# Twelve float32 units for eighteen, eight weight blocks ahead for fourteen, and two small operations moved to other engines

## The chip, the cores and the metric

The kernel runs on one core of one Trainium2 chip. The metric is the device time in microseconds (us). Every number of the profile is of one profiled execution of the kernel before; engines are named TensorE (PE; its weight loads PEld), VectorE (DVE), ScalarE (ACT), GpSimd (POOL) and SyncE (SP), which issues most transfers.

## The reference

Attention with a sliding window and a few sinks, then a two-layer feed-forward over its output:

```python
def _attn_ref(q, k, v, n_sink, window):        # (4, 8, 768, 64); 4 sinks, window 128
    scores = scale * np.matmul(q, k.transpose(0, 1, 3, 2))
    keep = is_sink | in_window                  # pos_k < n_sink, or 0 <= pos_q - pos_k < window
    scores = np.where(keep, scores, -1000000000.0)
    a = np.exp(scores - np.max(scores, axis=-1, keepdims=True))
    a = a / (np.sum(a, axis=-1, keepdims=True) + 1e-09)
    return np.matmul(a, v)

def _moe_ref(x, w_in, w_out):                   # (3072, 512) @ (512, 2048), @ (2048, 512)
    h = x @ w_in
    g = np.where(h >= 1, h, np.where(h <= -1, 0.0, (h + 1) ** 2 / 4))
    return g @ w_out
```

All arrays are float32, except that the weights come as 64-bit floats, which the kernel decodes itself.

## The kernel before

**Units and chunks.** A unit is one batch, one head and three blocks of 128 queries: 64 units in all. Eight units (the heads of one batch and one half of the sequence) make a chunk, whose 384 rows of attention output, `xn`, are the input of one feed-forward. There are eight chunks. While the feed-forward of one chunk runs, the units of the next go through attention. The first stage therefore has attention alone, the last feed-forward alone.

**A unit's four steps** follow each other in the list that `attn_steps` makes, one unit behind the next. `load` fetches q and k. `scores` makes three score blocks of 128 x 260 (two neighbouring key blocks and four sinks), takes their row maxima on VectorE (L236, the custom operation, with the mask) and the exponential with the sums on ScalarE (L239); then it adds 1e-9 to the three sums (L244), takes the reciprocal (L245) and scales the rows (L257 on ScalarE, L259 on VectorE). `transp` transposes the probabilities on TensorE (L312, L314; L324, L325) and copies them back. `av` multiplies them by v (L378). `values` fetches v.

**Two kinds of units.** The first `NATIVE` = 18 units are "native": q, k, probabilities and v are plain float32, which TensorE takes in two rows per matmul. The others are split for float32r: each number is written as a rounded high part (ScalarE: L214, L217, L283, L288) and a remainder (a subtraction: L216, L218, L284, L289), and the matmul is done with both. L218, L284 and L289 are on GpSimd; the remainder of k, L216, is on VectorE, but on GpSimd for the units in `KL_POOL`. Split units add the previous block's probabilities (L251), form the remainder of the transposed probabilities (L329, L331), mask it into two triangles on GpSimd (L334, L336: the affine selections), spread the sinks (L338), and add two halves of the output (L383, L384). Native units need none of this; instead they have a second group of transposes, more rows in `av`, and a copy of the transposed sinks (L320).

**Weights.** 32 blocks (w_in and w_out in turn, 128 x 512 each) are fetched as 64-bit words and decoded by four rows on VectorE (L147, L148, L149, L151) and one on ScalarE (L150). The first `WFIRST` = 14 blocks are interleaved with the first stage, in the list that the program is written from; the other 18 with the first feed-forward.

**The feed-forward** goes through 16 blocks of 128 hidden columns: `stage1` (L416, 12 matmuls), the activation (L423, L424 on ScalarE, L425 on VectorE, L426 on ScalarE, then the remainder `gl`, L427: on GpSimd in the first feed-forward, on VectorE in the others), and `stage2` (L435, 9 matmuls), which runs `LAG` = 2 blocks behind. Its input is split by L446 (ScalarE) and L447 (VectorE), four quarters each.

**What sets the order.** TensorE's rows stand in the order written by `spread`, which interleaves attention and feed-forward by estimated weights. On VectorE, ScalarE, GpSimd and SP a scheduler sets the order; each engine then works through its queue strictly in that order, so a row that waits holds up all behind it.

Of the kernel before, what the change touches and what calls it, by code (L numbers as in the profile page):

```python
# [13 lines left out]
ALU = mybir.AluOpType  # L14
# [3 lines left out]
P = 128  # L18
NT = S // P
CT = 3  # L20
NSINK = 4
# [2 lines left out]
QK = CT * P + P + CT * KB  # L24
NJ = DFF // P

NATIVE = 18


KL_POOL = range(18, 20)  # L30
GL_POOL = 0
NORM = "vaa"


CHECK = range(24, 24 + 2 * NJ)
WFIRST = 14
AHEAD = 3
SYNC = 8

# [10 lines left out]
def attn_ffn(ctx, tc, qk, vx, vs, par, w_in, w_out, out):  # L50
    nc = tc.nc
# [64 lines left out]
    for r0 in (0, 32):  # L116
        r = r0 + CT * NSINK
# [77 lines left out]
    def load(u):  # L195
        b, h, t0 = u
        T = CT * P
        W = (P if t0 else -NSINK) + CT * KB
        if units.index(u) < NATIVE:

# [13 lines left out]
        nc.scalar.copy(k_s, k_r)  # L214
        eng = nc.gpsimd if units.index(u) in KL_POOL else nc.vector
        eng.tensor_tensor(k_s[D:P], k_r[D:P], k_s[D:P].bitcast(F32), op=ALU.subtract)  # L216
# [4 lines left out]
    def scores(u, i):  # L221
        b, h, t0 = u
        qs, k_s = st["qk", u]
        if i == 0:
            st["p", u] = [att.tile([P, CT, 260], F32, name="p"), att.tile([P, 2 * CT], F32, name="stat")]
        p, stat = st["p", u]
        t = t0 + i
        lo = KB if t == 0 else 0
        c0 = i * KB if t0 else max(0, (i - 1) * KB)
        ps = ps_a.tile([P, 512], F32, name="ps_a")  # L230
        for j, q in enumerate(qs):
            nc.tensor.matmul(ps[:, lo:260], lhsT=q[:, i * P:(i + 1) * P], rhs=k_s[:, c0:c0 + 260 - lo],  # L232
                             start=(j == 0), stop=(j == len(qs) - 1))
        peak_i = peak[:, units.index(u), i:i + 1]
        m = m0 if t == 0 else (m1 if t == 1 else m2)
        nc.vector.tensor_tensor_reduce(  # L236
            out=p[:, i, lo:260], in0=ps[:, lo:260], in1=m, scale=-0.0625 if units.index(u) < NATIVE else -0.125, scalar=3.0e38,
            op0=ALU.add, op1=ALU.min, accum_out=peak_i)
        nc.scalar.activation(p[:, i, lo:260], p[:, i, lo:260], AF.Exp, bias=peak_i, scale=-1.0,  # L239
                             accum_out=stat[:, i:i + 1])  # L240
        if i < CT - 1:
            return
        st.pop(("qk", u))
        nc.vector.tensor_scalar(stat[:, CT:2 * CT], stat[:, 0:CT], 1.0e-9, None, op0=ALU.add)  # L244
        nc.vector.reciprocal(stat[:, CT:2 * CT], stat[:, CT:2 * CT])  # L245
        i0 = int(t0 == 0)
        c0 = 0
        if units.index(u) >= NATIVE:

            c0 = P  # L250
            nc.vector.tensor_tensor(p[:, i0:, KB:260], p[:, i0:, KB:260], p[:, i0:, 0:P], op=ALU.add)  # L251
        for i in range(CT):
            lo = KB if t0 + i == 0 else c0
            r = stat[:, CT + i:CT + i + 1]
            eng = NORM[i] if units.index(u) < NATIVE else "v"
            if eng == "a":
                nc.scalar.activation(p[:, i, lo:260], p[:, i, lo:260], AF.Copy, scale=r)  # L257
            else:
                (nc.gpsimd if eng == "p" else nc.vector).tensor_scalar(p[:, i, lo:260], p[:, i, lo:260], r, None,  # L259
                                                                       op0=ALU.mult)  # L260
        if units.index(u) < NATIVE:
            sk = None
        else:
            sk = att.tile([P, CT * NSINK], F32, name="sk")[:, :(CT - i0) * NSINK]
            nc.vector.tensor_copy(sk.rearrange("p (i s) -> p i s", s=NSINK), p[:, i0:, P:KB])
        st["p", u] = (p, sk)

    def values(u):
        b, h, t0 = u
        kb0 = max(t0 - 1, 0)  # L270
        nb = t0 + CT - kb0
        if units.index(u) < NATIVE:
            v_s = att.tile([P, 4, 2, D], F32R, name="v_s").bitcast(F32).rearrange("p n a d -> p (n a) d")[:, :nb]
# [19 lines left out]
    def transp(u, part):  # L293
# [4 lines left out]
        ns = CT - i0  # L298
        r = ns * NSINK
        spt = sp[units.index(u) % 2]  # L300
        ps = ps_a.tile([P, 512], F32, name="ps_a")
# [6 lines left out]
        if units.index(u) < NATIVE:  # L308
            c, blk = ((0, 0), (1, KB))[part]
            i0 = i0 * (1 - part)  # L310
            for i in range(i0, CT):
                nc.tensor.transpose(ps[:, i * P:(i + 1) * P], p[:, i, blk:blk + P], ident)  # L312
                if not part:
                    nc.tensor.transpose(ps[:NSINK, (i - 1) * CT * P:((i - 1) * CT + 1) * P], p[:, i, P:KB], ident)  # L314
            nc.scalar.copy(pth.bitcast(F32)[:, i0:, c], ps[:, i0 * P:T].rearrange("p (i q) -> p i q", q=P))  # L315
            if part:
                st.pop(("p", u))
            else:
                spt = st["sp", u] = spn[units.index(u) % 2]
                nc.vector.tensor_copy(spt[:NSINK].rearrange("r (t q) -> r t q", q=P)[:, :ns],  # L320
                                      ps[:NSINK].rearrange("r (t q) -> r t q", q=P)[:, ::CT])
            return
        for i in range(CT):
            nc.tensor.transpose(ps[:, i * P:(i + 1) * P], p[:, i, KB:260], ident)  # L324
# [181 lines left out]
    ps = ps_a.tile([P, 512], F32, name="ps_a")  # L506
# [56 lines left out]
    with tc.If(other_v > 0):  # L563
        with tc.tile_pool(name="gen", bufs=1) as gen:
# [9 lines left out]
            for t0 in (0, CT):  # L574
                keep = gen.tile([P, CT, S], F32, name="keep")
                kidx = gen.tile([P, S], I32, name="kidx")
                r = gen.tile([P, S], F32, name="r")
# [53 lines left out]
```

## Time and profile before

| | us |
|---|---|
| median of 3 runs (742.02 to 743.75) | 743.18 |
| the profiled execution | 744.81 |
| its span, first to last instruction | 743.0 |
| TensorE matmuls busy (3867 rows) | 709.9 |
| VectorE busy (1456 rows) | 535.2 |
| ScalarE busy (1301 rows) | 505.0 |
| GpSimd busy (446 rows) | 267.9 |

The page's chain of waits (the work that ended last, followed back) gives TensorE 61% of the span, VectorE 20%, ScalarE 8%. The busy time of matmuls is modelled at its end, so a TensorE at 100% can still hide short waits. In the 40 slices of the span (18.6 us each) the busy tenths are

```profile
PE   5889999999999999999989999999999999999996
DVE  7998994346877787878877888878888677842221
ACT  4887776566767877777767876778676675544342
POOL 2101312313544454535445454645545444410000
```

A digit is the busy share of a slice in tenths. The first feed-forward matmul starts at 61.4 us, the second feed-forward's at 157.4.

### The profile page before, as it was taken

What the parts mean: (1) busy time and instruction counts of PE and PEld (TensorE: products, weight loads), DVE (VectorE), ACT (ScalarE), POOL (GpSimd) and SP (SyncE); (2) the same over time, 40 slices, a digit from 0 to 9 for tenths busy, and PEclk for the clock granted to TensorE, in tenths of its full rate; (3) what the DMA queues carried; (4) which work ended last, traced back from release to release, by engine and by line L of the source; (5) the groups of instructions that cost most, each with busy time, mean ns of one, the idle gap of its engine ahead of it and who ended that gap; (6) DMA issues with size and microseconds to landing.
All of it is one profiled execution on the core that took longest, in us unless ns stands there. A gap on an engine that the chain in (4) does not pass through costs nothing.

```text
span 743.0 us, 12353 instructions
## 1 busy us (share of the span) xinstructions
PE 709.9 (96%) x3867; PEld 622.9 (84%) x3867; DVE 535.2 (72%) x1456; ACT 505.0 (68%) x1301; POOL 267.9 (36%) x446
## 2 busy tenths in 40 slices
PE   5889999999999999999989999999999999999996
PEld 3446888888998998999879998899888999989995
DVE  7998994346877787878877888878888677842221
ACT  4887776566767877777767876778676675544342
POOL 2101312313544454535445454645545444410000
PEclk9999999999999999999999999999999999999999
DMA  8876541221232443434424433415322120001001
GB/s 271 279 242 222 199 132 59 55 70 41 58 104 77 145 123 112 122 100 128 123 73 123 149 105 95 121 64 166 123 84 67 61 81 26 9 1 44 1 0 48
DMA packets 43211, 76.20 MB, mean 103 GB/s; under 512 B 7298, under 2 KB 27778, under 8 KB 43138
## 3 DMA queue, kind: packets, MB, share of 16 engines
q1 hardware_dynamic: 39682, 62.75, 27.4%
q10 hardware_dynamic: 3456, 12.58, 4.9%
q8 instruction: 33, 0.54, 0.3%
q14 instruction: 40, 0.33, 0.2%
HBM read 69.02 MB, written 6.29 MB: 101 GB/s over the span
## 4 chain that ended last, share of the span: by engine, by line
PE 61%; DVE 20%; ACT 8%; DMA 4%; issue 3%; POOL 2%; SPq 0%; ACTq 0%; POOLq 0%
PE o_ps L435 24%; PE h_ps L416 24%; PE ps_a L378 6%; PE ps_a L232 3%; DVE k_s L216 3%; DVE p L259 3%; ACT p L239 2%; DVE gl L427 2%; ACT k_s L214 2%; DVE pt L329 1%; DMA r<-qk 1%; DVE p L251 1%; DVE g L425 1%; DVE p L236 1%; PE ps_a L324 1%
## 5 line engine op out<-in xcount | busy, mean ns | idle before, releaser
L416 PE MATMUL h_ps<-x,wi 128*128 128x384 f32 x1536 | 311.1, 341 | 0.6 <-DVE x L447 0.6
L416 PEld LDWEIGHTS h_ps<-x,wi 128*128 128x128 f32 x1536 | 263.1, 188 | 10.5 <-issue 1.9
L435 PE MATMUL o_ps<-w,gh 128*128 128x512 f32 x768 | 244.5, 399 | 0.0
L435 PE MATMUL o_ps<-w,gl 128*128 128x512 f32 x384 | 151.2, 394 | 0.0
L435 PEld LDWEIGHTS o_ps<-w,gh 128*128 128x128 f32 x768 | 134.5, 188 | 16.6 <-issue 1.9
L425 DVE SCALAR_TENSOR_TENSOR g<-g,h_ps 128x384 f32<-128x384 f32 x128 | 70.2, 548 | 70.4 <-ACT g L424 69.8
L239 ACT ACTIVATE p<-p,peak 128x260 f32<-128x260 f32 (+1 forms) x192 | 94.0, 490 | 35.5 <-DVE peak L236 34.4
L423 ACT ACTIVATE g<-h_ps,half 128x384 f32<-128x384 f32 x128 | 73.7, 576 | 57.7 <-PE h_ps L416 56.4
L426 ACT CAST gh<-g 128x384 fp32r<-128x384 f32 x128 | 65.5, 511 | 60.7 <-DVE g L425 59.8
L218 POOL TENSOR_TENSOR q_l<-r,q_h 128x384 fp32r<-128x384 f32 x46 | 46.8, 1018 | 129.8 <-ACT q_h L217 123.0
L236 DVE CUSTOM_DVE_ANT_0 p<-ps_a,m 128x260 f32<-128x260 f32 (+1 forms) x192 | 74.2, 398 | 20.9 <-PE ps_a L232 19.9
L435 PEld LDWEIGHTS o_ps<-w,gl 128*128 128x128 f32 x384 | 72.0, 188 | 17.6 <-POOL gl L427 0.2
L427 DVE TENSOR_TENSOR gl<-g,gh 128x384 fp32r<-128x384 f32 x112 | 67.9, 606 | 26.1 <-ACT gh L426 25.2
L232 PE MATMUL ps_a<-k_s,q_h 128*128 128x260 f32 (+1 forms) x246 | 70.2, 335 | 15.7 <-DVE sk L331 7.6
L216 DVE TENSOR_TENSOR k_s<-k_r,k_s 64x524 fp32r<-64x524 f32 (+1 forms) x44 | 47.5, 1079 | 44.2 <-ACT k_s L214 44.2
L378 PE MATMUL ps_a<-pt,v_s 128*128 128x256 f32 (+2 forms) x402 | 69.9, 298 | 1.8 <-ACT pt L315 1.2
L232 PEld LDWEIGHTS ps_a<-k_s,q_h 128*128 128x128 f32 x246 | 45.5, 198 | 30.5 <-issue 11.4
L424 ACT ACTIVATE g<-g 128x384 f32<-128x384 f32 x128 | 67.1, 524 | 2.8
L336 POOL TENSOR_SCALAR_AFFINE_SELECT pt<-pt 128x384 fp32r<-128x384 f32 (+1 forms) x92 | 51.5, 560 | 45.0 <-DVE pt L329 36.4
L378 PEld LDWEIGHTS ps_a<-pt,v_s 128*128 128x128 f32 (+1 forms) x402 | 57.8, 176 | 11.7 <-issue 1.6
L259 DVE TENSOR_SCALAR p<-p,stat 128x132 f32<-128x132 f32 (+1 forms) x156 | 60.4, 433 | 0.3
L334 POOL TENSOR_SCALAR_AFFINE_SELECT pt<-pt 128x384 fp32r<-128x384 f32 (+1 forms) x92 | 49.1, 534 | 30.2 <-ACT pt L328 30.2
(108 smaller groups left out, 899.4 us busy)
## 6 DMA issues: line engine op xcount, KB each, us to landing
r<-qk SPq DMA_DIRECT2D x46, 192.0 KB
k_r<-qk SPq DMA_DIRECT2D x32, 262.0 KB
again<-w_in SPq DMA_DIRECT2D x16, 512.0 KB
again<-w_out SPq DMA_DIRECT2D x16, 512.0 KB
w<-w_in ACTq DMA_DIRECT2D x12, 512.0 KB
w<-w_out ACTq DMA_DIRECT2D x12, 512.0 KB
out<-o SPq DMA_DIRECT2D x23, 256.0 KB
r<-vx SPq DMA_DIRECT2D x32, 128.0 KB
```

The lines of the kernel that those rows point to most:

```text
L216: eng.tensor_tensor(k_s[D:P], k_r[D:P], k_s[D:P].bitcast(F32), op=ALU.subtract)
L232: nc.tensor.matmul(ps[:, lo:260], lhsT=q[:, i * P:(i + 1) * P], rhs=k_s[:, c0:c0 + 260 - lo], start=(j == 0), stop=(j == len(qs) - 1))
L236: nc.vector.tensor_tensor_reduce(out=p[:, i, lo:260], in0=ps[:, lo:260], in1=m, scale=-0.0625 if units.index(u) < NATIVE else -0.125, scal ...
L239: nc.scalar.activation(p[:, i, lo:260], p[:, i, lo:260], AF.Exp, bias=peak_i, scale=-1.0, accum_out=stat[:, i:i + 1])
L259: (nc.gpsimd if eng == "p" else nc.vector).tensor_scalar(p[:, i, lo:260], p[:, i, lo:260], r, None, op0=ALU.mult)
L378: nc.tensor.matmul(z, lhsT=w, rhs=y, start=(n == 0), stop=(n == len(mms) - 1))
L416: nc.tensor.matmul(h_ps[:, :T], lhsT=w_i[j][:, w, ct * P:(ct + 1) * P], rhs=x[:, y, ct], start=(ct == 0 and n == 0), stop=(ct == NCT - 1 a ...
L423: nc.scalar.activation(g, h_ps[:, :T], AF.Relu, bias=half, scale=0.5)
L424: nc.scalar.activation(g, g, AF.Square)
L425: nc.vector.scalar_tensor_tensor(g, g, 1.0, h_ps[:, :T], op0=ALU.min, op1=ALU.max)
L427: (nc.gpsimd if row0 == GL_POOL else nc.vector).tensor_tensor(gl, g, gh.bitcast(F32), op=ALU.subtract)
L435: nc.tensor.matmul(o_ps[tt], lhsT=gg[:, tt * P:(tt + 1) * P], rhs=w_o[j][:, w], start=(j == 0 and n == 0), stop=(j == NJ - 1 and n == 2))
```

## The change

Four edits. `NATIVE` falls from 18 to 12, so units 12 to 17 are split for float32r. `KL_POOL` becomes the range 12 to 18, so the remainder of k of those six units is on GpSimd, and that of units 18 and 19 moves to VectorE. `WFIRST` falls from 14 to 8, so in the written list six more blocks are decoded during the first feed-forward. The copy of the transposed sinks, L320, goes from VectorE to ScalarE, and the addition of 1e-9, L244, from VectorE to GpSimd, for all 64 units.

```diff
--- before.py
+++ after.py
@@ -24,16 +24,16 @@
 QK = CT * P + P + CT * KB
 NJ = DFF // P
 
-NATIVE = 18
-
-
-KL_POOL = range(18, 20)
+NATIVE = 12
+
+
+KL_POOL = range(12, 18)
 GL_POOL = 0
 NORM = "vaa"
 
 
 CHECK = range(24, 24 + 2 * NJ)
-WFIRST = 14
+WFIRST = 8
 AHEAD = 3
 SYNC = 8
 
@@ -241,7 +241,7 @@
         if i < CT - 1:
             return
         st.pop(("qk", u))
-        nc.vector.tensor_scalar(stat[:, CT:2 * CT], stat[:, 0:CT], 1.0e-9, None, op0=ALU.add)
+        nc.gpsimd.tensor_scalar(stat[:, CT:2 * CT], stat[:, 0:CT], 1.0e-9, None, op0=ALU.add)
         nc.vector.reciprocal(stat[:, CT:2 * CT], stat[:, CT:2 * CT])
         i0 = int(t0 == 0)
         c0 = 0
@@ -317,8 +317,8 @@
                 st.pop(("p", u))
             else:
                 spt = st["sp", u] = spn[units.index(u) % 2]
-                nc.vector.tensor_copy(spt[:NSINK].rearrange("r (t q) -> r t q", q=P)[:, :ns],
-                                      ps[:NSINK].rearrange("r (t q) -> r t q", q=P)[:, ::CT])
+                nc.scalar.copy(spt[:NSINK].rearrange("r (t q) -> r t q", q=P)[:, :ns],
+                               ps[:NSINK].rearrange("r (t q) -> r t q", q=P)[:, ::CT])
             return
         for i in range(CT):
             nc.tensor.transpose(ps[:, i * P:(i + 1) * P], p[:, i, KB:260], ident)
```

**VectorE, end of the first stage**, up to the last of the four quarters of the feed-forward's input (L447). `stat` are the sums, `spn` the sinks, `p` the probabilities, `peak` the maxima, `o` and `wi`/`w` the decode's words and results. Before:

```order
L245 RECIPROCAL stat_681<-stat_681 128x3
L320 COPY spn0_141<-ps_a_708 4x256
L147 TENSOR_SCALAR o_863<-w_699 128x512
L236 ISA p_735,peak_100<-ps_a_737,m0_111 128x128
L236 ISA peak_100 128x1
L259 TENSOR_SCALAR p_680<-p_680,stat_681 128x128
L151 TENSOR_TENSOR w_808<-o_809,w_808 128x512
L148 SCALAR_TENSOR_TENSOR o_863<-w_699,o_863 128x512
L236 ISA p_735,peak_100<-ps_a_761,m1_110 128x260
L236 ISA peak_100 128x1
L147 TENSOR_SCALAR o_925<-w_741 128x512
L447 TENSOR_TENSOR x_727<-xn_167,x_727 128x384
```

and now:

```order
L148 SCALAR_TENSOR_TENSOR o_944<-w_826,o_944 128x512
L245 RECIPROCAL stat_639<-stat_639 128x3
L151 TENSOR_TENSOR w_909<-o_910,w_909 128x512
L149 SCALAR_TENSOR_TENSOR o_944<-w_826,o_944 128x512
L259 TENSOR_SCALAR p_638<-p_638,stat_639 128x128
L236 ISA p_684,peak_100<-ps_a_686,m0_111 128x128
L236 ISA peak_100 128x1
L147 TENSOR_SCALAR o_979<-w_866 128x512
L236 ISA p_684,peak_100<-ps_a_713,m1_110 128x260
L236 ISA peak_100 128x1
L447 TENSOR_TENSOR x_676<-xn_167,x_676 128x384
```

The rows L244 and L320 are gone from the queue; the block decoded last in front of L447 is `w_808`, the sixteenth, before, and `w_909`, the fourteenth, now. The reciprocal L245 now follows a row of GpSimd.

**GpSimd, start of the first feed-forward.** `gl` are the remainders of the activation, one for each of the 16 blocks; `k_s`, `q_l` are the remainders of a unit's k and q. Before, the queue is:

```order
L427 TENSOR_TENSOR gl_785<-g_783,gh_784 128x384
L427 TENSOR_TENSOR gl_834<-g_832,gh_833 128x384
L427 TENSOR_TENSOR gl_855<-g_853,gh_854 128x384
L427 TENSOR_TENSOR gl_944<-g_942,gh_943 128x384
L427 TENSOR_TENSOR gl_1001<-g_999,gh_1000 128x384
L427 TENSOR_TENSOR gl_1072<-g_1070,gh_1071 128x384
```

and now:

```order
L244 TENSOR_SCALAR stat_639<-stat_639 128x3
L216 TENSOR_TENSOR k_s_849<-k_r_848,k_s_849 64x392
L218 TENSOR_TENSOR q_l_846<-r_851,q_h_847 128x384
L244 TENSOR_SCALAR stat_685<-stat_685 128x3
L427 TENSOR_TENSOR gl_725<-g_723,gh_724 128x384
L427 TENSOR_TENSOR gl_772<-g_770,gh_771 128x384
L427 TENSOR_TENSOR gl_812<-g_810,gh_811 128x384
L216 TENSOR_TENSOR k_s_1009<-k_r_1008,k_s_1009 64x392
L218 TENSOR_TENSOR q_l_1006<-r_1011,q_h_1007 128x384
L244 TENSOR_SCALAR stat_861<-stat_861 128x3
L427 TENSOR_TENSOR gl_886<-g_884,gh_885 128x384
L427 TENSOR_TENSOR gl_955<-g_953,gh_954 128x384
```

The subtractions of the first split units and the additions to their sums stand among the gl rows; the first gl comes behind the q and k of unit 12 and the sums of unit 10.

**GpSimd, a unit of a later stage** (L176 is a one-element copy that holds back a fetch of the weights for a later check; `pt` are transposed probabilities). Before:

```order
L218 TENSOR_TENSOR q_l_5135<-r_5140,q_h_5136 128x384
L176 COPY again_5130<-peak_100 1x1
L334 AFFINE_SELECT pt_5059<-pt_5059 128x3x128
L336 AFFINE_SELECT pt_5059<-pt_5059 128x3x128
L334 AFFINE_SELECT pt_5059<-pt_5059 128x3x128
```

and now (another unit, since numbers shift):

```order
L218 TENSOR_TENSOR q_l_4025<-r_4030,q_h_4026 128x384
L176 COPY again_3980<-peak_100 1x1
L244 TENSOR_SCALAR stat_3874<-stat_3874 128x3
L334 AFFINE_SELECT pt_3912<-pt_3912 128x3x128
L336 AFFINE_SELECT pt_3912<-pt_3912 128x3x128
L334 AFFINE_SELECT pt_3912<-pt_3912 128x3x128
```

The addition stands behind the next unit's q remainder and the copy, and ahead of the selections of the previous unit.

## Rows read from the trace of the kernel before

**Rows 1.** Windows: stretch; busy (rows) of TensorE, its loads, VectorE, ScalarE, GpSimd; clock, DMA.
```profile
10.00:61.40 51.40, 39.88 (x179) 23.75 (x180) 50.33 (x161) 40.49 (x120) 2.01 (x2) 0.97 0.79 270
61.40:100.00 38.60, 37.97 (x204) 31.77 (x204) 37.59 (x94) 30.25 (x77) 10.27 (x6) 1.00 0.60 202
100.00:157.40 57.40, 57.40 (x300) 47.70 (x299) 29.05 (x78) 36.52 (x92) 13.63 (x14) 1.00 0.19 56
```

**Rows 2.** Timeline of VectorE, 51.8 to 53.8 us: start, duration, engine, line, operation.
```profile
51.76 0.67 DVE L151 TENSOR_TENSOR wi<-o,wi 128x512 fp32r<-128x512 f32 x1
52.36 0.67 DVE L148 SCALAR_TENSOR_TENSOR o<-w,o 128x512 int32<-128x512 int32 x1
52.96 0.40 DVE L320 COPY spn<-ps_a 4x256 f32<-4x256 f32 x1
53.30 0.41 DVE L147 TENSOR_SCALAR o<-w 128x512 int32<-128x512 int32 x1
53.63 0.15 DVE L244 TENSOR_SCALAR stat<-stat 128x3 f32<-128x3 f32 x1
```

**Rows 3.** Groups by form, VectorE: rows, busy us, mean ns, idle before.
```profile
L251 DVE TENSOR_TENSOR p<-p 128x256 f32<-128x256 f32 x14 | 5.8, 413 | 0.0
L259 DVE TENSOR_SCALAR p<-p,stat 128x132 f32<-128x132 f32 x124 | 50.6, 457 | 0.1
L329 DVE TENSOR_TENSOR pt<-ps_a,pt 128x384 fp32r<-128x384 f32 x46 | 24.4, 530 | 0.0
```

**Rows 4.** Timelines of VectorE, then GpSimd, 389 to 391 us (a later unit).
```profile
389.35 1.10 DVE L216 TENSOR_TENSOR k_s<-k_r,k_s 64x524 fp32r<-64x524 f32 x1 [2.75 <-ACT k_s L214]
390.47 0.51 DVE L244 TENSOR_SCALAR stat<-stat 128x3 f32<-128x3 f32 x1
390.89 0.54 DVE L251 TENSOR_TENSOR p<-p 128x384 f32<-128x384 f32 x1
...
389.82 0.66 POOL L176 COPY again<-peak 1x1 f32<-1x1 f32 x1
390.44 0.51 POOL L334 TENSOR_SCALAR_AFFINE_SELECT pt<-pt 128x384 fp32r<-128x384 f32 x1
```

**Rows 5.** Timeline of VectorE: the eighth L425, and the eighth L447.
```profile
106.29 0.55 DVE L425 SCALAR_TENSOR_TENSOR g<-g,h_ps 128x384 f32<-128x384 f32 x1
...
155.40 0.55 DVE L447 TENSOR_TENSOR x<-xn,x 128x384 fp32r<-128x384 f32 x1
```

**Rows 6.** Groups by form, ScalarE: the copy from PSUM.
```profile
L315 ACT COPY pt<-ps_a 128x256 f32<-128x256 f32 x18 | 6.4, 355 | 0.5 <-PE ps_a L314 0.5
```

**Rows 7.** Timeline of GpSimd: its first gl.
```profile
69.71 3.05 POOL L427 TENSOR_TENSOR gl<-g,gh 128x384 fp32r<-128x384 f32 x1 [43.48 <-ACT gh L426]
```

**Rows 8.** Line 427 (ns min/median/max, first and last start); then groups by form, GpSimd.
```profile
L427 POOL TENSOR_TENSOR gl<-g,gh x16: 1002/1017/3047, 69.7 to 157.0; 128x384 fp32r<-128x384 f32 x16
...
L218 POOL TENSOR_TENSOR q_l<-r,q_h 128x384 fp32r<-128x384 f32 x46 | 46.8, 1018 | 129.8 <-ACT q_h L217 123.0 <-PE ps_a L325 3.5 <-PE ps_a L324 3.0
L336 POOL TENSOR_SCALAR_AFFINE_SELECT pt<-pt 128x256 fp32r<-128x256 f32 x28 | 13.7, 490 | 13.8 <-DVE pt L329 11.0 <-DVE sk L265 1.6 <-DVE stat L245 1.0
L284 POOL TENSOR_TENSOR v_s<-r,v_s 128x192 fp32r<-128x192 f32 x14 | 8.3, 594 | 4.3 <-ACT v_s L283 4.2
```

**Rows 9.** Chain (start, us, what), native unit; then timeline of TensorE, float32r unit.
```profile
110.50 1.66 PE ps_a L378 x8
...
67.02 0.33 PE ps_a L312 x3
...
253.91 0.76 PE L378 MATMUL ps_a<-pt,v_s 128*128 128x256 f32 x5
...
254.62 0.39 PE L435 MATMUL o_ps<-w,gh 128*128 128x512 f32 x1
```

**Rows 10.** Waits of TensorE, then of SP: us, times, longest.
```profile
PE ps_a L232 <- DVE sk L331: 7.6, 9, 1.5
...
SPq L280 <- POOL q_l L218: 115.2, 43, 8.9
```


## Prediction

> **What bounds the kernel now.** I read the page's 40 slices and chain of waits first, then the windows by stage, then the timelines where two engines meet. Three regimes show. From 10 to 61.4 us (eight heads' attention, no feed-forward matmul yet) VectorE is busy 50.33 of 51.40 us and ScalarE 40.49, TensorE waits [rows 1]: VectorE sets the start. From 61.4 to 100 us, while the first feed-forward runs and the rest of the weights are decoded, VectorE is still busy 37.59 of 38.60. From 100 to 157.4 it is busy only 29.05 of 57.40 and TensorE all of it: there TensorE sets the end, and 28.3 us of VectorE are spare.
>
> **Prices on a full VectorE queue** are read from start to start [rows 2]: a decode row L148 or L151 0.60 us, L149 like them (same duration as L148's 0.67 in its form), L147 0.33, so a block 2.13; the sinks' copy L320 0.34; the add L244 0.07. Generally a row costs its duration less 0.07.
>
> **Fewer blocks ahead, the copy and the add gone from VectorE.** WFIRST 14 to 8 sounds like six blocks, 12.8 us. The order says less: ahead of the fourth L447, where the feed-forward's input is complete, 16 blocks were finished and now 14. Less there: two L147, two L148, one L149, two L151 (3.7 us), nine L320 (3.1), ten L244 (0.7): 7.5 us. Ahead of the eighth L425, the end of the stretch in which VectorE sets the pace: decode 3.3, thirteen L320 4.4, fourteen L244 1.0, small rows 0.5, against 1.9 of new rows of float32r units: 7.3 us less.
>
> Ahead of the eighth L447 (the next stage's input) all blocks stand in both. Seventeen L320 and eighteen L244 are gone (7.1), and new are 6 L251 at 0.34, 12 L259 at 0.39, 5 L329 and 4 L383 at 0.46 (L383 priced like L329) [rows 3], 2 L216 at 1.03 ([rows 4]), and 15 small ones (L265, L331, L384), at most 0.34 each, I take 0.2: 16.1 in, so +9.0 us by then. In the trace the eighth L425 ends at 106.8 and the eighth L447 at 155.9 [rows 5].
>
> ScalarE takes the copy. Its form isn't in the trace; the nearest row, L315's copy of 128x256 from PSUM, is 0.355 [rows 6], so 0.2 to 0.36, I take 0.29: nine copies are 2.6 us, less 1.2 for two casts. ScalarE's 40.5 us would then stand in a stretch of about 44 us. It is hidden only just; if ScalarE binds there, I price the start at 5 us less instead of 7.5.
>
> **Six units to float32r: GpSimd.** These units put their subtractions and triangular selections on GpSimd, amid the decode. The first of its rows there, a gl subtraction, takes 3.05 us [rows 7] where the median of the 16 is 1.02 [rows 8]: it gets in only when VectorE's decode lets it. To the eighth gl the GpSimd queue gains 8 L216 and L218 at 1.02, 4 adds, one L284 at 0.59 and 4 selections at 0.49 [rows 8] (L216 priced as L218): 11.6 us. To the sixteenth: 10 of the 1.02 kind, 8 adds, 6 L284, 20 selections, 9 more small ones at L284's price: 30.4 us. The add on GpSimd is not in the trace: from the 0.07 it costs on VectorE to the 0.66 of a 1x1 copy beside a VectorE subtraction [rows 4]; I take 0.2.
>
> What a microsecond of GpSimd takes from VectorE is bounded by 0 and 1. In [rows 4] L244 lasts 0.51 where it lasts 0.15 in [rows 2] alone, with a selection started beside it: 0.36 lost to some 0.5. I take a half. The Trainium skill, "SBUF — State Buffer", section "Who interferes with whom", says that VectorE rows with two SBUF inputs, and tensor_scalar in its two-port modes, and GpSimd share one port pair under an exclusive lock, the later one waiting for the whole instruction. The 3.05 us agrees; the rule would put the loss near 1 in decode, where most rows have two SBUF inputs, and is the third rival below.
>
> So the eighth L425 comes 7.3 less 5.8 (half of 11.6), 1.5 us earlier, at 105.3. From there to the eighth L447 VectorE has 9.0 + 7.3 = 16.3 us more of its own and half of 18.8, 9.4, for GpSimd: 25.7 of the 28.3 us spare. The spare is nearly used up: the mark comes 1.5 + 2.6 = 4.1 us earlier by VectorE's reckoning. I take **4**.
>
> **Six units to float32r: TensorE.** A native unit's value product takes 1.66 us, a float32r one 0.71 from its first matmul to the next work [rows 9]; of seven transposes four remain, three at 0.11 less (three take 0.33 in [rows 9]); the scores I take as equal, two matmul rows a block in either form. In the first feed-forward five of the six transpose groups and four of the value products fall: 5 x 0.33 + 4 x 0.95 = 5.4 us. With the start's 7.5 TensorE alone would allow 12.9, so 9 of it are idle, waiting for VectorE and GpSimd. Behind 157.4, where TensorE is never short of work, one group and two products remain: **2.2** us, all on the path.
>
> **The add in the 46 later units** (and the native ones, where GpSimd idles). Now: L216, L244 at 390.47, L251 at 390.89 [rows 4], the reciprocal behind. On GpSimd the add stands behind the next unit's q_l and ahead of the selections of the unit before, and is done while L216 or L251 runs; VectorE saves 0.42, or loses 0.24 where the add takes 0.66. What waits behind a late add: the reciprocal, and with it all of VectorE, then L259, the transposes, TensorE's next scores. TensorE's waits of that kind are 7.6 us in nine places [rows 10]; more than that can't be won. I take **1.5**; from 7.6 won to 9 lost (38 x 0.24).
>
> Loads: the six units fetch the same q, k and v, but through one buffer r in turn, so SP's v load waits for GpSimd's q_l (115.2 us in 43 places now [rows 10], 2.7 each) and the next unit's k_r stands behind it on SP. With a unit every 10 us that is hidden; if q_l comes late as in [rows 7], it adds 2 us to a unit, covered by the one-step lead.
>
> **Sum.** 4 + 2.2 + 1.5 = 7.7 us. The profiled execution took 744.81 (span 743.0, 1.8 around it), 1.6 above the median of 743.18; taken off the median this gives **735.5**.
>
> **Rivals.**
> First, TensorE keeps the lead: the port costs VectorE next to nothing and LAG's two blocks of slack absorb what's left. Then 5 to 7.5 of the start, 5.4, 2.2 and 1.5: 14 to 17 us, **728**. For it: TensorE never idles from 100 on, and gl is needed two blocks after it is made. Against: 3.05 us for one gl.
>
> Second, no change: the start gains 5, the first feed-forward gives it back, and the later adds cost what the 2.2 wins: **743**. For it: ScalarE nearly full; an in-order queue with one more waiting row. Against: 0.42 freed on VectorE in each unit.
>
> Third, the port pair, slower. GpSimd has 16 gl (15 us), 30 new and 4 old ones, 49 us, between some 56 us and the end of that stage. At the decode's price for it, 10.27 us for six gl [rows 1], 1.71 for 1.0, that is 84 us; with one fifth more in waits for casts and transposes, 105, ending at 161: 4 us later than 157.4. Then gl is late, TensorE stands in L435, and with 2.2 won behind it and the adds hidden badly the time is **746**. It decides where GpSimd's rows cost 1.6 times their plain duration up to the end of the stage, not only during the decode. By the skill's lock rule this is the outcome if decode spreads over the whole stage; the order ends it at the 12th of 16 L425, against it.
>
> **Chances.** Forecast 0.48, first rival 0.25, second 0.10, third 0.17. One measurement of this kernel tells 0.2% (1.5 us) from no change. Faster: nearly all of the forecast's share, the first rival's and a little of the second's: 0.74; same 0.10; slower 0.16. Range: from 726 (first rival, adds well hidden) to 746 (third); the forecast's own range is 731 to 740.
>
> **What would show it.** Right: the first L416 at 54 to 57 us; L244 on GpSimd near 0.2 us; gl rows of 2 to 3 us until the decode ends; VectorE busy over 90% up to about 150; the second feed-forward's first L416 near 153; later stages equal to within a microsecond. First rival: that L416 at 145 to 148. Third: waits of L435 for gl, and the L416 behind 158. Wrong altogether: the later stages moving by more than 2 us each, for I give the add almost nothing there.

## The result, and the profile after

The changed kernel takes 737.38 us (median of 10 runs, 733.75 to 739.27), the kernel before, measured beside it, 742.63 (741.80 to 743.75): ratio 0.9925, 95% interval 0.9907 to 0.9942. The forecast was 735.5. The profiled execution took 737.51 us, its span is 735.8 (before 743.0). The median differs by 5.3 us from that of the kernel before.

The busy tenths in 40 slices, with the granted TensorE clock as a last row, of the changed kernel:

```profile
PE   5889898899999999999999999999989999999996
DVE  8999999857786777878877887778887677842221
ACT  5997767567677867877767877778757766545332
POOL 3113567645452555636555555646556344500000
PEclk9999999999999999999999999999999999999998
```

GpSimd's digits rise in the fifth to eighth slice (74 to 147 us). VectorE stays at 8 or 9 to the eighth slice, where it had fallen to 4 in the seventh; TensorE has an 8 in slices 5, 7 and 8, where it had a 9.

Stages are read from one chunk's first L416 to the next one's (us):

| | start | first feed-forward | third stage | fourth to eighth | last | span |
|---|---|---|---|---|---|---|
| before | 61.4 | 96.0 | 84.6 | 425.9 | 75.2 | 743.0 |
| after | 54.4 | 102.5 | 81.6 | 422.1 | 75.2 | 735.8 |
| difference | -7.0 | +6.5 | -3.0 | -3.8 | 0 | -7.2 |

The spans differ by 7.2 us and the medians by 5.3, mostly because the profiled execution before took 744.81 us, 2.2 above the 742.63 given above. Two things in its start are not the work of the edits. The eight value products (L378) ahead of the first L416 ran at a granted clock of 0.50, so that they took 3.40 us up to that L416 (at 61.42) where they take 1.90 now (to 54.42). VectorE's first decode row, L147, waited for its weights until 9.84 us, and now until 8.97. The rows, before and then now, with the window of the low clock first (columns as in [rows 1]):

```profile
57.70:61.10 3.40, 3.40 (x11) 1.65 (x9) 2.68 (x7) 0.85 (x3) 0.00 (x0) 0.50 0.61 241
58.02 2.40 PE L378 MATMUL ps_a<-pt,v_s 128*64 128x128 f32 x6
60.20 1.04 PE L378 MATMUL ps_a<-spn,vsn 128*64 128x256 f32 x2
9.84 0.43 DVE L147 TENSOR_SCALAR o<-w 128x512 int32<-128x512 int32 x1 [1.51 <-DMA w<-w_in]
...
52.52 1.30 PE L378 MATMUL ps_a<-pt,v_s 128*64 128x128 f32 x6 [0.47 <-DVE peak L236]
53.65 0.59 PE L378 MATMUL ps_a<-spn,vsn 128*64 128x256 f32 x2
8.97 0.43 DVE L147 TENSOR_SCALAR o<-w 128x512 int32<-128x512 int32 x1 [0.66 <-DMA w<-w_in]
```

Less these 1.5 and 0.9 us, the start gains some 4.6 us and not 7.0; that is an estimate from these rows. Every comparison with the start of 61.4 below has to be read with this in mind.

Windows of the changed kernel (columns as in [rows 1]): the start, the first feed-forward up to 100 us, on to the end of the decode, and the rest of that stage:

```profile
10.00:54.40 44.40, 38.01 (x179) 22.33 (x180) 42.97 (x131) 41.16 (x128) 6.16 (x12) 1.00 0.86 292
54.40:100.00 45.60, 42.41 (x220) 35.46 (x219) 45.50 (x96) 33.65 (x84) 20.60 (x18) 0.96 0.53 177
100.00:130.50 30.50, 24.03 (x124) 20.66 (x123) 30.27 (x58) 19.56 (x53) 23.90 (x32) 0.94 0.31 89
130.50:156.90 26.40, 25.91 (x136) 23.45 (x137) 16.75 (x54) 16.78 (x46) 13.60 (x24) 0.94 0.17 46
```

Where [rows 1] had VectorE half idle from 100 us on, it is now full to 130.5, and TensorE, which never waited there, stands 6.5 of 30.5 us. Behind 130.5 VectorE is idle for 9.7 us: its spare time is at the wrong end. TensorE's longest waits for VectorE, in the whole program (us, times, longest):

```profile
PE ps_a L232 <- DVE sk L331: 4.3, 5, 1.4
PE ps_a L324 <- DVE peak L236: 4.3, 2, 3.7
PE ps_a L312 <- DVE peak L236: 3.6, 4, 2.8
PE ps_a L232 <- DVE xn L384: 3.5, 2, 3.1
```

The three long ones (2.8, 3.7 and 3.1 us) lie in the first feed-forward; the first row answers to the 7.6 us in nine places of [rows 10].

The wait that ends at 131 us, on TensorE (start, duration), then what VectorE did meanwhile, then GpSimd:

```profile
127.46 0.40 PE L435 MATMUL o_ps<-w,gl 128*128 128x512 f32 x1
130.99 0.56 PE L232 MATMUL ps_a<-k_s,q_h 128*128 128x260 f32 x1 [3.13 <-DVE xn L384]
...
127.82 0.18 DVE L245 RECIPROCAL stat<-stat 128x3 f32<-128x3 f32 x1
127.91 2.61 DVE L151 TENSOR_TENSOR w<-o,w 128x512 fp32r<-128x512 f32 x1
130.55 0.29 DVE L384 TENSOR_TENSOR xn<-ps_a,xn 64x128 f32<-64x128 f32 x1
...
128.06 0.40 POOL L336 TENSOR_SCALAR_AFFINE_SELECT pt<-pt 128x256 fp32r<-128x256 f32 x1
128.44 0.98 POOL L427 TENSOR_TENSOR gl<-g,gh 128x384 fp32r<-128x384 f32 x1
129.39 0.58 POOL L284 TENSOR_TENSOR v_s<-r,v_s 128x192 fp32r<-128x192 f32 x1
```

The decode row L151 takes 2.61 us where it takes 0.67 in [rows 2]: 1.94 too much. The three GpSimd rows beside it sum to 1.96, none slower than it is elsewhere. L384, which frees TensorE, stands behind L151 in VectorE's queue. The section of the Trainium skill that the prediction cites ("SBUF — State Buffer", "Who interferes with whom") has the blocked engine wait for the other's whole instruction. The trace agrees, and goes further: by these times VectorE's row stood through three in succession.

Behind each of the long waits TensorE ran at half its clock. Windows around the second one (clock in the third last column):

```profile
109.00:112.70 3.70, 0.05 (x1) 0.00 (x0) 3.70 (x10) 0.69 (x2) 2.05 (x3) 1.00 0.50 142
113.80:117.20 3.40, 3.40 (x13) 3.20 (x12) 3.40 (x7) 3.03 (x11) 2.86 (x5) 0.51 0.11 29
117.20:121.00 3.80, 3.80 (x23) 3.48 (x22) 3.74 (x12) 1.63 (x5) 2.79 (x6) 1.00 0.61 165
```

From 113.8 to 117.2 us the granted clock is 0.51, the lower level (1.2 GHz); the same shows from 86.4 to 89.8 and from 130.8 to 134.2. Half the speed for 3.4 us is 1.7 us lost, three times: 5.1. Before, no such stretch lay between 61.4 and 740 us; the one from 57.7 to 61.1 is named above.

### The profile page after: what moved, and what is told of

It is laid out like the page before. It is cut to its first block, busy times and chain, and to the rows that moved or that the text cites. A ratio compares the mean times of both kernels' runs of the same rounds, so it can differ in the third digit from the quotient of the medians.

```text
span 735.8 us, 12453 instructions
## 1 busy us (share of the span) xinstructions
PE 702.0 (95%) x3837; PEld 621.4 (84%) x3837; DVE 547.3 (74%) x1424; ACT 510.4 (69%) x1325; POOL 329.8 (45%) x562
## 4 chain that ended last, share of the span: by engine, by line
PE 58%; DVE 19%; ACT 8%; DMA 6%; issue 4%; POOL 3%; SPq 0%; ACTq 0%; POOLq 0%
PE o_ps L435 25%; PE h_ps L416 24%; PE ps_a L378 4%; PE ps_a L232 3%; DVE o L149 2%; DVE p L259 2%; ACT p L239 2%; DVE o L148 2%; DVE k_s L216 2%; DMA r<-qk 2%; DVE g L425 2%; PE ps_a L324 2%; DVE gl L427 1%; DMA r<-vx 1%; DVE p L236 1%
## 5 line engine op out<-in xcount | busy, mean ns | idle before, releaser
L416 PE MATMUL h_ps<-x,wi 128*128 128x384 f32 x1536 | 310.2, 341 | 0.4 <-DVE x L447 0.4
L416 PEld LDWEIGHTS h_ps<-x,wi 128*128 128x128 f32 x1536 | 263.8, 189 | 9.4 <-issue 0.8
L435 PE MATMUL o_ps<-w,gh 128*128 128x512 f32 x768 | 244.6, 399 | 0.0
L435 PE MATMUL o_ps<-w,gl 128*128 128x512 f32 x384 | 151.7, 395 | 0.0
L435 PEld LDWEIGHTS o_ps<-w,gh 128*128 128x128 f32 x768 | 135.2, 190 | 15.4 <-ACT pt L315 0.4
L218 POOL TENSOR_TENSOR q_l<-r,q_h 128x384 fp32r<-128x384 f32 x52 | 54.1, 1040 | 134.0 <-ACT q_h L217 109.5
L425 DVE SCALAR_TENSOR_TENSOR g<-g,h_ps 128x384 f32<-128x384 f32 x128 | 70.2, 548 | 58.8 <-ACT g L424 58.1
L427 DVE TENSOR_TENSOR gl<-g,gh 128x384 fp32r<-128x384 f32 x112 | 71.6, 639 | 24.4 <-ACT gh L426 23.4
L435 PEld LDWEIGHTS o_ps<-w,gl 128*128 128x128 f32 x384 | 72.5, 189 | 17.5
L236 DVE CUSTOM_DVE_ANT_0 p<-ps_a,m 128x260 f32<-128x260 f32 (+1 forms) x192 | 74.3, 400 | 15.5 <-PE ps_a L232 14.1
L216 DVE TENSOR_TENSOR k_s<-k_r,k_s 64x524 fp32r<-64x524 f32 (+1 forms) x46 | 47.5, 1032 | 47.7 <-ACT k_s L214 47.6
L232 PE MATMUL ps_a<-k_s,q_h 128*128 128x260 f32 (+1 forms) x228 | 66.1, 329 | 14.0 <-DMA k_s<-qk 4.8
L378 PE MATMUL ps_a<-pt,v_s 128*128 128x256 f32 (+2 forms) x396 | 66.1, 291 | 0.8 <-DVE peak L236 0.7
L336 POOL TENSOR_SCALAR_AFFINE_SELECT pt<-pt 128x384 fp32r<-128x384 f32 (+1 forms) x104 | 54.6, 526 | 25.6 <-DVE pt L329 22.5
L232 PEld LDWEIGHTS ps_a<-k_s,q_h 128*128 128x128 f32 x228 | 42.1, 199 | 28.3 <-issue 11.0
L378 PEld LDWEIGHTS ps_a<-pt,v_s 128*128 128x128 f32 (+1 forms) x396 | 58.2, 181 | 7.8 <-DVE peak L236 2.3
L259 DVE TENSOR_SCALAR p<-p,stat 128x132 f32<-128x132 f32 (+1 forms) x168 | 62.9, 424 | 0.2
L334 POOL TENSOR_SCALAR_AFFINE_SELECT pt<-pt 128x384 fp32r<-128x384 f32 (+1 forms) x104 | 56.6, 544 | 8.1 <-ACT pt L328 3.1
```

What stands on the lines that cost most here:

```text
L236: nc.vector.tensor_tensor_reduce(out=p[:, i, lo:260], in0=ps[:, lo:260], in1=m, scale=-0.0625 if units.index(u) < NATIVE else -0.125, scal ...
L378: nc.tensor.matmul(z, lhsT=w, rhs=y, start=(n == 0), stop=(n == len(mms) - 1))
L416: nc.tensor.matmul(h_ps[:, :T], lhsT=w_i[j][:, w, ct * P:(ct + 1) * P], rhs=x[:, y, ct], start=(ct == 0 and n == 0), stop=(ct == NCT - 1 a ...
L425: nc.vector.scalar_tensor_tensor(g, g, 1.0, h_ps[:, :T], op0=ALU.min, op1=ALU.max)
L427: (nc.gpsimd if row0 == GL_POOL else nc.vector).tensor_tensor(gl, g, gh.bitcast(F32), op=ALU.subtract)
L435: nc.tensor.matmul(o_ps[tt], lhsT=gg[:, tt * P:(tt + 1) * P], rhs=w_o[j][:, w], start=(j == 0 and n == 0), stop=(j == NJ - 1 and n == 2))
```

## The experiments

The kernel before was measured again beside each group of runs, with medians of 742.6 to 743.9 us; each ratio is to the one beside it.

Theory: VectorE's queue, read row by row, sets the start; in the first feed-forward the split units' GpSimd rows stretch VectorE's decode rows, and TensorE pays for that in single waits and in clock behind them. Rivals: the units cost the same wherever they lie; GpSimd's own queue is what is late; WFIRST or a lucky order decides.

### One edit at a time

**The add alone.** Only L244 goes to GpSimd.

```diff
-        nc.vector.tensor_scalar(stat[:, CT:2 * CT], stat[:, 0:CT], 1.0e-9, None, op0=ALU.add)
+        nc.gpsimd.tensor_scalar(stat[:, CT:2 * CT], stat[:, 0:CT], 1.0e-9, None, op0=ALU.add)
```

> The kernel before with only the add of 1e-9 on GpSimd. Theory A: start and first feed-forward within 1 us of before; the stages behind 157 are together 3 to 4 us shorter, as the changed kernel's were beyond what the six units explain: 739 to 740. Rival: the later stages' gain came from something else (the six units' shift of the queues), then 742 to 744. If the add, at 0.55 us for 0.15, were a loss on GpSimd: 745 or more.

Measured: 735.23 us, ratio 0.9883 (0.9859 to 0.9906), twice what I expected, so none of the three holds as stated. The first feed-forward gives 1.0 us (95.0). The start is 57.4 us, though nothing but some ten adds left VectorE's written order: the scheduler now finishes 14 blocks ahead of the fourth L447, as in the changed kernel, where it finished 16. Two blocks at 2.13 us and ten adds at 0.07 are 5.0; measured 4.0 against the start of 61.4, which holds some 2 us of that one execution. The third to eighth stages give 4.0 us in sum. TensorE's wait of [rows 10] in this kernel:

```profile
PE ps_a L232 <- DVE sk L331: 4.6, 3, 2.7
```

3.0 us of 7.6 are gone, six of nine places: that is most of the 4.0.

**The add and the copy.** L320 goes to ScalarE as well.

```diff
-                nc.vector.tensor_copy(spt[:NSINK].rearrange(...
+                nc.scalar.copy(spt[:NSINK].rearrange(...
```

> The kernel before with two edits: the add of 1e-9 on GpSimd and the sinks' copy on ScalarE (18 native units, WFIRST 14). Nine sinks' copies (3.1 us) leave VectorE's queue ahead of the fourth L447, but the scheduler now finishes 15 blocks there, one more than with the add alone (14). Theory A, the start is VectorE's queue counted row by row: 57.4 us (add alone) less 3.1, plus 2.1 for the block, gives a first L416 at 56 to 57 us; later stages as with the add alone; time 733.5 to 735.5, so that the rest of the gain of the kernel with all three small edits (733.0) is WFIRST's. Theory B, ScalarE's rows hold the start up: first L416 at 57.5 us or later, time 736 or more. Theory C, the copy alone is what brought 735.2 to 733.0: time 732 to 733.5 with a first L416 below 55.

Measured: 733.29 us, 0.9865 (0.9847 to 0.9883); first L416 at 55.1 us, a little better than theory A's count. ScalarE doesn't hold the start up (B falls).

**The three small edits**, 18 native units: WFIRST 8 besides.

```diff
-WFIRST = 14
+WFIRST = 8
```

> The kernel before with WFIRST 8, the sinks' copy on ScalarE and the add on GpSimd, and 18 native units as before. Theory A: the first feed-forward starts at 54 to 56 us, the gain is kept through that stage because GpSimd has only the gl rows there: the second starts at 150 to 152, no TensorE wait above 1 us in it; in all 733 to 736, at least as fast as the whole change. Theory B (later decode costs): the second feed-forward starts at 156 to 158, in all 740 to 742.

Measured: 733.0 us, 0.9852 (0.9828 to 0.9875): 0.3 from the kernel without the third edit. This kernel's theory A holds in the time (the second feed-forward begins at 149.4 us), and B falls. For the kernel with the add and the copy, C comes nearest (its start was to be below 55 us): the copy brought the 2 us, and WFIRST nothing that can be measured.

**The units alone**, on the kernel before.

```diff
-NATIVE = 18
-KL_POOL = range(18, 20)
+NATIVE = 12
+KL_POOL = range(12, 18)
```

> The kernel before with only NATIVE 12 and KL_POOL 12 to 18. Theory A (GpSimd's rows of six more split units take VectorE's time through the shared port, VectorE is late and TensorE waits): the first feed-forward's first matmul stays near 61 us as before, the second's comes later than 157.4, near 162, with TensorE waits of 2 to 4 us behind VectorE rows between 80 and 135 us; the third stage is 2 to 3 us shorter; in all 745 to 748. Theory B (the six units pay by TensorE's 5.4 us and the loss came from the later decode): the second feed-forward starts 3 to 5 us earlier than 157.4, in all 735 to 738.

Measured: 743.9 us, 1.0008 (0.9994 to 1.0021), between the theories. The third stage gains 3.1 us (81.4), but the first feed-forward is 99.0 for 96.0. The start is 58.0 us for 61.4, which no theory had. The rows on VectorE ahead of the last value products are the same in number as before (14 finished blocks, eight copies, nine adds); what differs is that no low clock and no wait for the first weights lie in it:

```profile
8.25 0.42 DVE L147 TENSOR_SCALAR o<-w 128x512 int32<-128x512 int32 x1
56.09 1.30 PE L378 MATMUL ps_a<-pt,v_s 128*64 128x128 f32 x6
```

So these rows show nothing of the edit's in the earlier start, and the second feed-forward begins at 157.0 us, 0.4 earlier than before. Behind a wait of 2.4 us for L236 (ending at 90.9 us), and behind two of 1.0 us (ending at 114.0 and 115.5), the clock is low (0.57 from 92 to 96 and from 116 to 120). On top of the other three edits the same edit costs 737.4 - 733.0 = 4.4 us, or 5.4 by the two ratios.

**The change with WFIRST at 14.**

```diff
-WFIRST = 8
+WFIRST = 14
```

> The changed kernel with WFIRST back at 14. Ahead of the fourth L447 the order has 15 finished blocks for 14, ahead of the eighth L425 28 for 27. Theory A: one more block ahead moves the start by 1 to 2 us, to 56, and takes as much off the first feed-forward: within 1.5 us of the changed kernel, 736 to 739. Theory B: the decode that is done later is what costs, then the first feed-forward is 3 us or more shorter and the whole 733 to 735.

Measured: 735.27 us, 0.989 (0.9869 to 0.9911), at the border of both theories. The start is 54.4 us as with 8, not 56, and the first feed-forward takes 100.9. The 2.1 us against 737.38 do not come back in the last run below, so I take them for a difference in order, not for the worth of WFIRST.

### Does shared access cost the time?

Both kernels add work on GpSimd to the changed kernel in units 12 to 17, behind the remainder of q; one reads and writes a scratch tile, the other only writes it.

```diff
+        if units.index(u) < 18:
+            nc.gpsimd.tensor_copy(scrap[0:1, 0:1], q_l[0:1, 0:1].bitcast(F32))
+            for _ in range(3):
+                nc.gpsimd.tensor_tensor(scrap[:, 300:600], scrap[:, 0:300], scrap[:, 0:300], op=ALU.subtract)
```

> The changed kernel with more work on GpSimd that the result doesn't need: in each of the units 12 to 17, behind the remainder of q, a 1x1 copy and three subtractions of 128x300 that read a scratch tile twice and write it, some 2.4 to 3 us a unit plain, 15 to 18 in all. Theory A, shared access: such rows take about 0.6 us of VectorE's time for each of their own while VectorE is full; four of the six units lie there, so VectorE loses 6 to 8 us, the decode ends 5 us or more later than 130.5 and the first feed-forward grows by 4 to 9 us (106 to 111), time 741 to 746; at least 3 us more than the twin whose additional rows only write. Theory B, GpSimd's own queue: what costs is that gl and the selections stand behind more rows; then this kernel and its twin grow alike. Theory C, GpSimd has room: both within 1.5 us of the changed kernel (737.4).

```diff
+            for _ in range(4):
+                nc.gpsimd.memset(scrap[:, 0:600], 0.0)
```

> The twin of the kernel before it: in each of the units 12 to 17 a 1x1 copy and four fills of 128x600 on GpSimd, some 2.4 to 3 us a unit plain, which write the scratch tile but read nothing. Theory A, shared access by reading rows: VectorE hardly loses anything, the decode ends within 2 us of 130.5, the first feed-forward grows by at most 2 us, time 736 to 740. Theory B, GpSimd's own queue: it grows as its twin does, within 1.5 us. Theory C: both within 1.5 us of 737.4.

Measured: reading 745.47 us, 1.0028 (1.0006 to 1.0049), that is 8.1 more than the changed kernel; writing 737.97, 0.9921 (0.9897 to 0.9945), 0.6 more. The added rows from 54 to 131 us (min/median/max ns, first and last start), reading, then writing:

```profile
L224 POOL TENSOR_TENSOR scrap<-scrap x15: 675/1027/1198, 63.6 to 127.0; 128x300 f32<-128x300 f32 x15
...
L224 POOL MEMSET scrap<- x20: 589/600/761, 64.8 to 127.5; 128x600 f32 x20
```

Fifteen rows against twenty in the same stretch: the reading ones are stretched by half beside a full VectorE, the writing ones hardly. The Trainium skill ("SBUF — State Buffer", "Who interferes with whom") says that two-input VectorE rows collide with GpSimd rows that read SBUF, not with those that only write; both runs agree. The times, 8.1 us against 0.6, speak against theories B and C. Theory A holds in the times and in the first feed-forward of the reading kernel (109.9 us), but not in the end of the decode, which it had at 135.5 or later for the reading kernel and within 2 us of 130.5 for the writing one. One reservation: the scheduler orders VectorE's queue differently in the three kernels, and in the profile of the writing one the decode ends no earlier (133.9 us) than in the reading one (133.1). The five groups of decode rows sum to 61.1 us with the reading rows, 58.7 with the writing ones and 60.1 in the changed kernel, while TensorE's waits in that stage sum to 16.2, 9.4 and 10.0 us. The rows show the sharing; that it alone makes the 8.1 us is not separated from the order.

### How many split units?

The changed kernel with other numbers of native units N (and `KL_POOL` from N to 18), in the order in which they ran:

```diff
-NATIVE = 12
-KL_POOL = range(12, 18)
+NATIVE = 15
+KL_POOL = range(15, 18)
```

> The changed kernel with 15 native units in place of 12 (units 15 to 17 split, their k remainder on GpSimd). Theory A, the split units cost the first feed-forward time because GpSimd's rows slow VectorE down while it still decodes and TensorE waits for that: units 12 to 14 are the ones that fall into the decode, so most of the loss goes: the first feed-forward from 102.5 to 96 to 98.5 us, the third stage about 1.5 us longer than 81.6, time 732 to 734.5, at or near the 733.0 of the kernel with all 18 native. Theory B, every split unit costs the same: halfway between 733.0 and 737.4, 735 to 736, with a first feed-forward near 99. Theory C, native units' extra work on TensorE is what counts: 737.5 or more.

Measured: 727.47 us, 0.9786 (0.9765 to 0.9808); first feed-forward 94.7 us, third stage 82.0. That is some 5 us better than theory A, which had the direction right; B and C fall.

N = 14:

> The changed kernel with 14 native units. Theory A: a split unit costs where its GpSimd rows and its new VectorE rows fall into the decode, and gains on TensorE (about 1.3 us: a transpose group and a shorter value product) where they don't. In the kernel with 15 native units the first split rows come at 96 us and the decode ends at 115; unit 14's come some 10 us earlier, its selections still inside: it loses 2 to 4 and gains 1.3, so 728.5 to 731, between 15 native (727.5) and 12 (737.4) but nearer to 15. Theory B, the 727.5 was a lucky order of VectorE's queue: 14 native lands anywhere from 732 to 737.

Measured: 726.80 us, 0.9774 (0.9743 to 0.9806). Theory B falls, and A was too high: the loss of 2 to 4 us that it gave unit 14 did not come.

N = 16:

> The changed kernel with 16 native units. Theory A: unit 15's rows come as the decode ends, so its loss was small, and TensorE, which sets the end there, gets 1.3 us more work: 728 to 730. Theory B, a lucky order in the kernel with 15 native units: nearer to the 733.0 of 18 native, 731 to 733.

Measured: 729.13 us, 0.9802 (0.9767 to 0.9836): theory A.

N = 13:

> The changed kernel with 13 native units. Theory A: units 13 and 14 both lie in the decode: 731 to 735, with at least one stretch of TensorE at half its clock behind a wait for VectorE, and a first feed-forward of 97 to 100.5 us. Theory B: the loss is that of unit 12 alone (the first one beside the fullest decode): 729 to 731 and no such stretch.

Measured: 733.35 us, 0.9871 (0.9836 to 0.9907); first feed-forward 98.3 us: theory A, but no stretch at half the clock in that stage.

N = 15 with WFIRST at 14:

> 15 native units with WFIRST at 14, as in the kernel before. Theory A: the scheduler, not WFIRST, decides where the blocks stand; 15 blocks in place of 14 ahead of the fourth L447 put the start 1 to 2 us later and the decode's end as much earlier: 727 to 729.5. Theory B: WFIRST 14 is the better setting by what it gave with 12 native units (735.3 for 737.4): 725 to 726.5.

Measured: 727.70 us, 0.9791 (0.9757 to 0.9824): theory A in the time: WFIRST makes no difference. The start, at 55.7 us for 55.6, did not come 1 to 2 us later, although one more block is finished ahead of the fourth L447.

In one row: 18 native 733.0, 16 729.1, 15 727.5, 14 726.8, 13 733.4, 12 737.4. Each split unit from the end of the list gains 0.7 to 2 us, until the fifth and sixth cost 6.5 and 4.0. The intervals of 16, 15 and 14 overlap, so which of these three is best is not shown. The windows of the whole decode, each from that kernel's first L416 to its last L151, show why; 18, 14, 13 and 12 native:

```profile
53.60:113.70 60.10, 59.81 (x317) 49.32 (x317) 56.76 (x130) 45.41 (x119) 13.66 (x15) 1.00 0.54 181
...
52.90:114.70 61.80, 58.09 (x309) 48.19 (x308) 60.29 (x127) 46.43 (x117) 24.51 (x22) 1.00 0.51 169
...
57.10:123.00 65.90, 59.78 (x315) 49.06 (x314) 65.26 (x135) 47.31 (x118) 27.21 (x30) 1.00 0.48 159
...
54.40:130.50 76.10, 66.44 (x343) 56.12 (x342) 75.77 (x153) 53.21 (x136) 44.50 (x49) 0.96 0.44 142
```

With 18 native units VectorE still has 3.3 us free in the decode, with 14 still 1.5, with 13 and 12 next to nothing; GpSimd's work in the decode goes from 13.7 to 44.5 us. I read this as a process that feeds itself, since a longer decode takes in the rows of later units too; no run separates that. The longest decode rows' groups (rows | busy us, mean ns), with 18 native units, then in the changed kernel:

```profile
L149 DVE SCALAR_TENSOR_TENSOR o<-w,o 128x512 int32<-128x512 int32 x18 | 13.7, 763 | 0.1
L151 DVE TENSOR_TENSOR w<-o,w 128x512 fp32r<-128x512 f32 x10 | 6.8, 679 | 0.0
...
L149 DVE SCALAR_TENSOR_TENSOR o<-w,o 128x512 int32<-128x512 int32 x18 | 17.7, 985 | 0.0
L151 DVE TENSOR_TENSOR w<-o,w 128x512 fp32r<-128x512 f32 x10 | 10.8, 1079 | 0.0
```

All five decode groups together take 60.1 us for 47.7: 12.4 more beside 30.8 more of GpSimd. VectorE's whole busy time in these two windows grows by 19.0 us, so a third of it, 6.6 us, is not stretch but the split units' own new rows on VectorE. With 14 native units TensorE's longest wait for VectorE in this stage is 1.6 us, with 13 it is 1.5, but the waits sum to 8.2 us in ten places; neither shows the low clock in this stage:

```profile
PE ps_a L312 <- DVE peak L236: 2.8, 2, 1.6
...
PE ps_a L312 <- DVE peak L236: 2.4, 3, 1.0
PE ps_a L324 <- DVE peak L236: 2.0, 2, 1.5
```

The kernel with 14 native units beats both kernels: 726.8 us, 2.3% under the kernel before (1.9 to 2.6% by the interval).

## Why the prediction came out right, step by step

The total was 1.9 us off; a change of 7.7 us was forecast and one of 5.3 measured. That it came so near is luck: by the profiles the second feed-forward began 3.5 us later than forecast, and the stages behind its start gave 3.1 us more, so that the errors nearly cancelled. Of the prediction's own signs of being right only the first, the start at 54 to 57 us, came true.

**The start, -7.5: right in direction, too large.** The profiles give 7.0 (first L416 at 54.4 us), but some 2.4 of it lie in the one profiled execution before, as shown above. Against the start of 58.0 us of the kernel with the units alone, which has as many VectorE rows ahead as the kernel before, the gain is 3.6. The medians, 1.9 us closer together than the spans, would leave 5.1. So the term was worth between 3.6 and 5.1 us. The count goes up to the fourth L447, while the first L416 begins 2.2 us ahead of that row (54.4 and 56.6 us), behind the last value products; so the count was not of the row that TensorE waits for. For the three other kernels it gives 5.0, 5.9 and 8.1 us; measured from 61.4 they are 4.0, 6.3 and 7.8, measured from 58.0 only 0.6, 2.9 and 4.4. What the start did gain is not WFIRST's (with 14 it is 54.4 us too); with the add the scheduler moved two blocks, and the copy left the queue.

**The copy, 0.29 on ScalarE, hidden: right on the hiding.** It takes 0.36:

```profile
L320 ACT COPY spn<-ps_a x9: 345/357/358, 14.5 to 52.3; 4x256 f32<-4x256 f32 x9
```

**What a microsecond of GpSimd takes from VectorE, "a half": about right.** 12.4 us of decode for 30.8 of GpSimd is 0.4; with 14 native units it is 5.2 for 10.8, 0.5. It is no constant: the kernel with the reading rows has 10.2 more of GpSimd in its decode than the changed one, and only 1.0 more of decode rows. The eighth L425 was to come 1.5 us earlier; it came 1.2 earlier, at 105.13 for 106.29 ([rows 5]), with the reservation on the start:

```profile
105.13 0.54 DVE L425 SCALAR_TENSOR_TENSOR g<-g,h_ps 128x384 f32<-128x384 f32 x1
```

The gl rows on GpSimd were to take 2 to 3 us until the decode ends; the eleven of them have a median of 1.3.

**"The spare is nearly used up: the mark comes 4.1 us earlier": the step that failed.** The second feed-forward began at 156.9 us, 0.5 earlier, not 4. The step took all of VectorE's idle time between the eighth L425 and the eighth L447 as time that new rows can fill, so that VectorE alone would set the mark. Windows between the ends of these two rows, before and now:

```profile
106.84:155.95 49.11, 49.11 (x257) 41.03 (x256) 21.34 (x61) 30.83 (x80) 12.17 (x12) 1.00 0.18 52
...
105.67:155.46 49.79, 42.83 (x224) 38.33 (x223) 40.45 (x102) 32.07 (x87) 32.84 (x51) 0.93 0.24 67
```

VectorE's work grew by 19.1 us, less than the 25.7 forecast, and 9.3 us stayed idle, and still the mark hardly moved. VectorE was full to 130.5 us, not to 150; by then TensorE had waited three times, and behind that TensorE set the pace again. TensorE's idle time in the stage I had at 9 us; it was 10.1 (102.5 less 92.4 busy), 9.5 more than before. Its work I had 5.4 us shorter. Busy time fell from 95.4 to 92.4, but 5.1 of the 92.4 are what the low clock cost, so the work itself fell by some 8. The sum from 157.4 is then: 7.0 earlier by the start, 8.1 by the work, 9.5 later by idle time, 5.1 later by the clock, 0.5 earlier in all. The clock was in no term of my sum. The mark was missed by 3.5 us, or by some 6 if the 2.4 us of the one execution before are left out, and the clock's 5.1 are most of that.

**TensorE behind that stage, -2.2**: the third stage gave 3.0, in the units-alone kernel 3.1; the kernel with the three small edits has 84.0 there, so 2.4 of the 3.0 are the units'. The size was right.

**The add in later units, -1.5: mis-sized.** The fourth to eighth stages gave 3.8; alone, the add gave 3.5 there and 4.0 in the third to eighth. Its row on GpSimd is not near 0.2:

```profile
L244 POOL TENSOR_SCALAR stat<-stat x64: 226/549/887, 10.6 to 633.8; 128x3 f32<-128x3 f32 x64
```

The median is 0.55, above what it costs on VectorE in [rows 4], and still it gains: in all 46 later units it runs beside an L216 or L251 on VectorE instead of between them. The cap I took from [rows 10], 7.6 us, was sound; I should have taken half of it rather than a fifth. By my own list (later stages moving by more than 2 us) this step was wrong: the third and the sixth moved by 3.0 and 2.5.

**The rivals.** The first (TensorE keeps the lead) fails at 156.9 us. The third had the port pair right but the place wrong: TensorE waits in no L435 for gl, but for `peak` and `xn`, VectorE's rows behind a stretched L151. The second came near in the first feed-forward, which gave back 6.5 of the 7.0, and was wrong on the later stages. The direction of the change and its range held because of the add in the later units, which the prediction gave almost nothing.

## What to carry to other kernels

Spare time of an engine is worth only what lies ahead of the wait: sum its queue up to each row that another engine waits for, not over the stage. Work put on GpSimd beside two-input VectorE rows cost VectorE some 0.4 to 0.5 of itself in the kernels with 12 and 14 native units, and only 0.1 where reading rows were added to the first of these, so the price has to be measured in place. The number of such units has a best range (14 to 16 native units here, with 6.5 us lost from 14 to 13), so it is worth stepping through. Before stages of two profiles are subtracted, compare each profiled execution with its median, and look for a low clock or a late transfer in it. Where a scheduler sets the order, a small edit may move large ones: read the order before crediting an edit.

## What the runs showed of the hardware that was not expected

A VectorE row with two inputs took 2.61 us for 0.67 beside three GpSimd rows in succession. After waits of 2.8, 3.7 and 3.1 us TensorE ran 3.4 us each at half the clock; after single ones of up to 1.6 us in the first feed-forward of the kernels with 13 and 14 native units it did not, yet one of 2.3 us in a later stage of the kernel with 14 (ending at 360.0 us, low from 361.3 to 364.7) was followed by such a stretch, and so were two of 1.0 us, 1.5 us apart, in the units-alone kernel; what decides there stays open. A GpSimd row of 128x3 takes 0.23 us at best and 0.55 in the median.
